# Scales of the expert weights: one per expert, surveyed one expert ahead, in place of one for all experts

## The chip, the cores and the metric

The kernel runs on one core of a Trainium2 chip. The metric is device time in microseconds (us) of one execution, lower is better. Five engines work side by side, each through its own instructions in order: PE (TensorE, matrix products; its weight loads are shown as PEld), DVE (VectorE), ACT (ScalarE), POOL (GpSimd) and SP, which here only issues DMA transfers. An instruction waits on semaphores for what it reads and for the buffers that it overwrites, and everything queued behind it on its engine waits with it.

## What is computed

Attention, a dense layer with a cosine, and a mixture of eight experts with a Sinkhorn gate, over 4 x 576 = 2304 tokens of width 512:

```python
scores = q @ k.T / 8 + decay;  x = softmax(scores, causal) @ v      # 4 x 8 heads of 64
h = x @ w_in;  x = (h * cos(h)) @ w_out                             # 512 -> 2048 -> 512
P = exp(x @ w_gate - max)                                           # 2304 x 8
for _ in range(8):
    P /= P.sum(1, keepdims=True) + 1e-9
    P /= P.sum(0, keepdims=True) + 1e-9
    P *= N / E
for e in range(8):
    out += P[:, e:e+1] * (max(x @ w1[e], 0) @ w2[e])                # 512 -> 1024 -> 512
```

## The kernel before

**Stages.** Attention fills the first 238 us, the dense layer the time to 654.7, the experts the rest. The experts' products are made of sums of submatrices (seven products in place of eight), in float16 with a high and a low part. So that the float16 parts neither overflow nor vanish, weights and activations are multiplied by powers of two: `scales["w1"]`, `scales["w2"]` for the weights of all experts together, `scales["x0"]` to `["x2"]` for the three thirds of the tokens. `backs` holds the inverses, and the last step of the gate's normalisation multiplies them into the gate.

**The survey in the dense stage.** The scale of `w1` needs the largest magnitude of all of `w1`, so both tensors are read once before the experts start: 128 chunks of 128 x 512 float32 (256 KB), loaded by `load_chunk` (L773) on SP into two buffers in turn (`seen` and `u`), and looked at by `survey` (L777, the instruction L779) on ACT: an absolute value with a running sum into one column of `found`, which bounds the magnitude from above. ACT also makes half of each sine of the dense layer. `find_scale` (L785, put in its places by `schedule_scale`, L804) reduces `found` to one number: a reduction on DVE, a transpose on PE (L791), a reduction, a product with ones on PE (L795) that spreads the number over the partitions, and four small DVE operations (L796 to L801). It takes two PSUM banks for that from three (`ps_h`, name "h") that the first products of the dense layer, L174, also use in turn. The same function serves the three thirds of the tokens.

**The experts.** Sixteen blocks follow each other: expert e = 0 to 7, and for each the two halves hb of its hidden width. A block runs over three pairs of token tiles in the order 0, 1, 2 or 2, 1, 0. A pair is two first layers (`first_layer`, L1314: seven products of six matmuls each, L1304, with one slot behind each product) and one second layer (`second_layer`, L1388: seven products of 24 matmuls, L1425, with two slots behind each). That makes 28 slots a pair and 84 a block. In a first layer three products accumulate in the same bank `y`, and ACT copies the bank to `ct` in between (L1320), while DVE adds (L1324) and forms the low parts (L1330), ACT the high parts (L1327, L1337, L1338), POOL further low parts (L1333, L1339).

**The plan.** What isn't a product of the block itself is set by hand: `put_at(n, ...)` hangs a function on slot n, counted through all blocks, and `hook()` behind each product issues what hangs there. `plan_weights` (L1472) hangs the preparation of the next block's four weight sets: `w_scale` (L1059, on ACT, in place), the sums on POOL (L1085), the high parts on ACT (L1114), the low parts on POOL (L1125), and the load of a later set on SP (`load_raw`, L1039). `plan_groups` (L1450) hangs the sums and parts of the token blocks of pairs 1 and 2 in block 0; those use four rooms `xs0` to `xs3` of 128 x 384. `keep_blocks` (L1021, slot 52 of block 0) stores the seven blocks `xc` of pair 2 to DRAM, `fetch_blocks` (L1025) brings them back behind the first layers of each block. The gate's normalisation (`sinkhorn`) is hung on the first slots of blocks 0 and 1 in small steps.

## Time and profile before

| what | us |
|---|---|
| runs | 1996.81, 1990.7, 1992.62 |
| median of the runs | 1992.62 |
| profiled execution, its own time | 1994.5 |
| its span in the profile | 1992.8 |
| granted clock of PE, mean | 0.999 |
| PE busy | 1953.8 (98%) |
| DVE, ACT, POOL busy | 1498.4, 1175.6, 1102.1 |

In the trace the dense stage runs from 238 to 654.7, block 0 from 654.7 to 746.5 (its third pair from 718.39), block 1 to 835.1; each of the blocks 3 to 15 takes 82.2 us. The names of the code appear in the rows without their numbers. A row "A x, us | idle" gives the busy time of a group, the mean time of one instruction in ns, and the idle time of its engine just before it with what ended most of it. The times in a row of the timeline are its start and its length, and in brackets stands how long the engine had been idle and what released it. A row of windows gives for one stretch the busy time of each engine with the count of its instructions, the granted clock of PE (1.00 is 2.4 GHz), the share of time that the DMA engines were busy, and GB/s.

### The profile page before, as it was taken

Reading aid. Unit: us, or ns where it says so; the run is one execution under the profiler, and the core shown is the slowest. Engines: PE = TensorE matmul, PEld = TensorE weight load, DVE = VectorE, ACT = ScalarE, POOL = GpSimd, SP = SyncE. Lnnn points to the kernel's source line nnn. Section 1 sums busy time; section 2 is a strip of 40 time slices with the busy share of each in tenths; the row PEclk is TensorE's granted clock in tenths of the full one; section 3 lists DMA queues with packets and bytes.
Section 4 is the critical chain, followed back from the end, with each engine's and each line's share of the span. In section 5 each row is a group of like instructions: output and inputs, shape, how many; then the busy total and the mean of one; then the engine's idle time right before and its main releaser. Section 6 shows DMA issues by size and latency. Waiting matters only on the chain.

```text
span 1992.8 us, 40081 instructions
## 1 busy us (share of the span) xinstructions
PE 1953.8 (98%) x15056; PEld 1544.5 (78%) x15056; DVE 1498.4 (75%) x3310; ACT 1175.6 (59%) x2481; POOL 1102.1 (55%) x1400
## 2 busy tenths in 40 slices
PE   7999999999999999999999999999999999999998
PEld 6888989898887676777777777777777777777776
DVE  8999788786666577787777777777777777777776
ACT  6888776656544675555555555655555555555543
POOL 7877455242166895555655546555465455565531
PEclk9999999999999999999999999999999999999999
DMA  5454255454321122112021120220212202122022
GB/s 124 111 111 103 67 183 171 134 157 142 97 62 45 44 88 77 49 61 88 22 78 62 48 88 27 80 72 31 88 33 77 78 22 88 33 78 78 12 88 64
DMA packets 142881, 157.58 MB, mean 79 GB/s; under 512 B 64608, under 2 KB 98784, under 8 KB 142688
## 3 DMA queue, kind: packets, MB, share of 16 engines
q1 hardware_dynamic: 142688, 155.04, 25.8%
q8 instruction: 118, 1.93, 0.4%
q14 instruction: 75, 0.61, 0.1%
HBM read 139.71 MB, written 10.37 MB: 75 GB/s over the span
## 4 chain that ended last, share of the span: by engine, by line
PE 85%; DVE 8%; ACT 3%; POOL 2%; issue 1%; DMA 0%; POOLq 0%; DVEq 0%; SPq 0%; ACTq 0%
PE y L1425 19%; PE y L1304 18%; PE bq L1425 14%; PE bq L1304 13%; PE a L829 7%; PE ph L174 6%; PE pv L598 2%; PE pst L548 2%; PE pss L491 1%; PE pss L492 1%; DVE acc L844 1%; DVE dm L134 1%; PE pv L578 1%; POOL w L135 1%; DVE xt L861 1%
## 5 line engine op out<-in xcount | busy, mean ns | idle before, releaser
L1425 PEld LDWEIGHTS <-h 128*128 128x128 f16 x6048 | 591.5, 98 | 76.1 <-POOL h L1339 1.2
L1304 PEld LDWEIGHTS <-wa 128*128 128x128 f16 x4032 | 394.8, 98 | 258.4 <-issue 5.0
L1304 PE MATMUL y<-xc,wa 128*128 128x384 f16 x2304 | 430.6, 326 | 1.8 <-ACT ct L1320 1.0
L1339 POOL TENSOR_TENSOR h<-rt,h 128x384 f16<-128x384 f32 x192 | 175.6, 915 | 452.2 <-ACT h L1338 444.9
L1425 PE MATMUL y<-wb,h 128*128 128x256 f16 x3456 | 408.9, 273 | 0.9 <-POOL h L1339 0.9
L1320 ACT ACTIVATE ct<-y 128x384 f32<-128x384 f32 x192 | 94.3, 491 | 423.1 <-PE y L1304 422.9
L1304 PE MATMUL bq<-xc,wa 128*128 128x384 f16 x1728 | 328.7, 327 | 0.2 <-ACT ct L1320 0.2
L1425 PE MATMUL bq<-wb,h 128*128 128x256 f16 x2592 | 306.7, 273 | 0.2 <-DVE h L1330 0.2
L1406 DVE SCALAR_TENSOR_TENSOR acc<-y,gate,acc 128x256 f32<-128x256 f32 x504 | 212.6, 477 | 48.6 <-PE y L1425 48.6
L829 PE MATMUL a<-H,w 128*128 128x512 f32 (+1 forms) x960 | 213.3, 370 | 4.0 <-DVE acc L844 2.6
L174 PE MATMUL ph<-xt,w 128*128 128x512 f32 (+1 forms) x960 | 211.5, 369 | 0.0
L829 PEld LDWEIGHTS a<-H,w 128*128 128x128 f32 x960 | 174.3, 188 | 30.4 <-issue 4.3
L174 PEld LDWEIGHTS ph<-xt,w 128*128 128x128 f32 x960 | 174.9, 188 | 22.8
L1406 DVE SCALAR_TENSOR_TENSOR acc<-bq,gate,acc 128x256 f32<-128x256 f32 x378 | 159.7, 478 | 39.2 <-PE bq L1425 39.1
L1330 DVE TENSOR_TENSOR h<-bq,h 128x384 f16<-128x384 f32 x288 | 158.1, 551 | 3.2 <-ACT h L1327 0.6
L1324 DVE SCALAR_TENSOR_TENSOR bq<-bq,ct 128x384 f32<-128x384 f32 x192 | 107.7, 561 | 65.4 <-PE bq L1304 64.6
L1324 DVE SCALAR_TENSOR_TENSOR bq<-y,ct 128x384 f32<-128x384 f32 x96 | 54.3, 566 | 122.8 <-PE y L1304 120.0
L1327 ACT CAST h<-bq 128x384 f16<-128x384 f32 x288 | 134.7, 483 | 14.2 <-DVE bq L1381 14.0
L1333 POOL TENSOR_TENSOR h<-st,h 128x384 f16<-128x384 f32 x96 | 88.1, 917 | 84.6 <-ACT h L1327 80.7
L194 ACT ACTIVATE t<-t,shift 128x512 f32<-128x512 f32 (+1 forms) x80 | 54.5, 681 | 89.1 <-DVE t L193 87.3
L1337 ACT ACTIVATE rt<-bq 128x384 f32<-128x384 f32 x192 | 93.8, 488 | 21.4 <-DVE bq L1324 18.8
L127 POOL TENSOR_SCALAR w<-dx 128x512 fp32r<-128x512 f32 x32 | 19.9, 623 | 154.0 <-DVE dx L126 153.1
(234 smaller groups left out, 3268.8 us busy)
## 6 DMA issues: line engine op xcount, KB each, us to landing
xc<-xd SPq DMA_DIRECT2D x105, 384.0 KB
sg<-in_moe_w_dram SPq DMA_DIRECT2D x64, 512.0 KB
seen<-in_moe_w_dram SPq DMA_DIRECT2D x64, 256.0 KB
u<-in_moe_w_dram SPq DMA_DIRECT2D x64, 256.0 KB
stg<-in_moe_w_in_dram SPq DMA_DIRECT2D x16, 512.0 KB
stg<-in_moe_w_out_dram SPq DMA_DIRECT2D x16, 512.0 KB
xd<-xc SPq DMA_DIRECT2D x14, 384.0 KB
q<-q SPq DMA_DIRECT2D x30, 160.0 KB
```

Source lines behind the costliest of these rows:

```text
L174: nc.tensor.matmul(ps[:, 0:n], w[:, ws, kk * P : (kk + 1) * P], XT[j][:, xs, kk, :], start=first, stop=kk == KD - 1 and (ws, xs) == PASSES ...
L829: nc.tensor.matmul(a_of[b, j][x][:, 0:n], w[:, s1, DM + x * P : DM + (x + 1) * P], H[:, s2, 0:n], start=i == 0 and n_ == 0, stop=end and n ...
L1304: nc.tensor.matmul(ps[:, 0:HN], w[:, ws, a, k, :], X[b][:, xs, k, :], start=fresh and n == 0, stop=n == 5, skip_group_check=not fresh,)
L1320: nc.scalar.activation(c, cut(ps), AF.Copy, scale=RAISE)
L1324: nc.vector.scalar_tensor_tensor(cut(c), cut(ps), RAISE, other, ALU.mult, ALU.add)
L1327: nc.scalar.copy(HT[m][c][:, 0, :], src)
L1330: nc.vector.tensor_tensor(HT[m][c][:, 1, :], src, HT[m][c][:, 0, :], ALU.subtract)
L1333: nc.gpsimd.tensor_tensor(HT[m][c][:, 1, :], src, HT[m][c][:, 0, :], ALU.subtract)
L1337: nc.scalar.activation(r, cut(ps), AF.Relu)
L1339: nc.gpsimd.tensor_tensor(HT[m][c][:, 1, :], r, HT[m][c][:, 0, :], ALU.subtract)
L1406: nc.vector.scalar_tensor_tensor(a, v, gate[:, tt, e : e + 1], a, ALU.mult, ALU.add)
L1425: nc.tensor.matmul(ps[:, at_ * HD : (at_ + 1) * HD], HT[m][a][:, s1, c * P : (c + 1) * P], W2T[side][m][:, s2, b, :], start=fresh and m == ...
```

## The change

Each expert has scales of its own for `w1` and `w2`. The dense stage surveys the 16 chunks of expert 0 alone; `share_most` and `set_scale` take the place of `find_scale` for the weights: the per-partition maxima (two numbers) are reduced on DVE, stored to DRAM, and read back to every partition (128 x 256 numbers), where one reduction and five small operations on DVE give the two scales and the factor that undoes them. The survey of expert e + 1 hangs on the slots of the first block of expert e: 16 looks on ACT and the loads of their chunks on SP, into the rooms `xs`, which are now two tiles of 128 x 768, of which a chunk takes 512 columns. In block 0 the looks stand on slots 53, 55, ..., 83, in the others on slots 2, 7, ..., 77. The maxima are shared at slot 2 of the block behind, the scale is set at its slot 8, and the gate's column of the expert is multiplied by the factor at its slot 10; for the experts 0 and 1 the gate's last step does it.

```diff
-        chunks = []
-        for x, src in enumerate(surveys):
-            for r in range(src.shape[0] // P):
-                chunks += [(x, src[r * P : (r + 1) * P, h, :]) for h in range(src.shape[1])]
-        NSEEN = len(chunks) // 2
...
-        scales = {nm: keep.tile([P, 1], F32, name=f"s{nm}") for nm in ("w1", "w2", "x0", "x1", "x2")}
-        backs = {nm: keep.tile([P, 1], F32, name=f"r{nm}") for nm in ("w1", "w2", "x0", "x1", "x2")}
-
-        def load_chunk(n):
-            if n < len(chunks):
-                nc.sync.dma_start(seen[n % 2], chunks[n][1])
-
-        def survey():
-            for n, (x, _) in enumerate(chunks):
-                nc.scalar.activation(
-                    seen[n % 2], seen[n % 2], AF.Abs, accum_out=found[x][:, n % NSEEN : n % NSEEN + 1]
-                )
-                load_chunk(n + 2)
+        scales = {nm: keep.tile([P, 1], F32, name=f"s{nm}") for nm in ("x0", "x1", "x2")}
+        backs = {nm: keep.tile([P, 1], F32, name=f"r{nm}") for nm in ("x0", "x1", "x2")}
+        wscale = [keep.tile([P, 2], F32, name=f"ws{x}") for x in range(2)]
+        wmost = keep.tile([P, 2], F32, name="wmost")
+        undo = keep.tile([P, NE], F32, name="undo")
+        sdram = ctx.enter_context(tc.tile_pool(name="sdram", bufs=1, space=bass.MemoryType.DRAM))
...
+        def look(e, n):
+            nc.scalar.activation(seen[n % 2], seen[n % 2], AF.Abs, accum_out=found[e % 2][:, n : n + 1])
+
+        def load_chunk(e, n):
+            if n < NSEEN:
+                nc.sync.dma_start(seen[n % 2], chunks_of(e)[n])
+
+        def survey(e):
+            for n in range(NSEEN):
+                look(e, n)
+                load_chunk(e, n + 2)
                 yield
+
+        def share_most(e, room):
+            nc.vector.tensor_reduce(
+                wmost, found[e % 2].rearrange("p (x n) -> p x n", x=2), axis=AX.X, op=ALU.max
+            )
+            nc.sync.dma_start(mostd[e], wmost)
+            nc.sync.dma_start(room, mostd[e].rearrange("p x -> (p x)").partition_broadcast(P))
+
+        def set_scale(e, room):
+            sc = wscale[e % 2]
+            nc.vector.tensor_reduce(wmost, room.rearrange("q (p x) -> q x p", x=2), axis=AX.X, op=ALU.max)
+            nc.vector.tensor_scalar(wmost, wmost, 2.0**-LIMIT, 2.0**LIMIT, ALU.max, ALU.min)
+            nc.vector.tensor_scalar(wmost.bitcast(I32), wmost.bitcast(I32), 0x7F800000, None, ALU.bitwise_and)
+            nc.vector.tensor_scalar(
+                sc.bitcast(I32), wmost.bitcast(I32), -1.0, float((254 + TOP) << 23), ALU.mult, ALU.add
+            )
+            nc.vector.tensor_scalar(wmost, wmost, 2.0**-TOP, None, ALU.mult)
+            nc.vector.scalar_tensor_tensor(
+                undo[:, e : e + 1], wmost[:, 0:1], 1.0 / RAISE, wmost[:, 1:2], ALU.mult, ALU.mult
+            )
+
+        def undo_gate(e):
+            g = gate[:, :, e]
+            nc.vector.tensor_scalar(g, g, undo[:, e : e + 1], None, ALU.mult)
...
-        load_chunk(0)
-        load_chunk(1)
-        looking[0] = survey()
-        PER = 2
-        schedule_scale("w1", found[0], NSEEN // PER + 1)
-        schedule_scale("w2", found[1], 2 * NSEEN // PER + 1, 3)
+        load_chunk(0, 0)
+        load_chunk(0, 1)
+        looking[0] = survey(0)
+        at(after_l2, 12, lambda: share_most(0, seen[0][:, 0 : 2 * P]))
+        at(after_l2, 18, lambda: set_scale(0, seen[0][:, 0 : 2 * P]))
...
-        xtmp = temps("xs", 4)
+        xs = [xp.tile([P, 2 * HN], F32, name=f"xs{c}") for c in range(2)]
+        xtmp = [t[:, c : c + HN] for t in xs for c in (0, HN)]
...
-            t, scale = stage_of(n), scales[ejobs[n][0]]
+            kind, e = ejobs[n][0:2]
+            which = 0 if kind == "w1" else 1
+            t, scale = stage_of(n), wscale[e % 2][:, which : which + 1]
...
-                    undo = small["gr"]
-                    nc.vector.scalar_tensor_tensor(undo, backs["w1"], 1.0 / RAISE, backs["w2"], ALU.mult, ALU.mult)
                     for p in range(NPR):
                         g = gate[:, p * TT : (p + 1) * TT, :]
-                        nc.vector.tensor_scalar(g, g, undo, backs[f"x{p}"], ALU.mult, ALU.mult)
+                        nc.vector.tensor_scalar(g, g, backs[f"x{p}"], None, ALU.mult)
+                    for e in range(2):
+                        undo_gate(e)
...
+        def plan_survey(blk):
+            e = blocks[blk][0] + 1
+            base = blk * NB
+            first, step = (53, 2) if blk == 0 else (2, 5)
+
+            def begin():
+                seen[:] = [t[:, 0:DM] for t in xs]
+                load_chunk(e, 0)
+                load_chunk(e, 1)
+
+            put_at(base + first - 2, begin)
+            for n in range(NSEEN):
+                put_at(base + first + step * n, lambda n=n: (look(e, n), load_chunk(e, n + 2)))
+            room = xs[0][:, DM : DM + 2 * P]
+            put_at(base + NB + 2, lambda: share_most(e, room))
+            put_at(base + NB + 8, lambda: set_scale(e, room))
+            if e > 1:
+                put_at(base + NB + 10, lambda: undo_gate(e))
...
+            if hb == 0 and e + 1 < NE:
+                plan_survey(blk)
```

On SP, around the stores of pair 2's blocks in block 0 (`xd2`; `sg` are the stages of the weights, `xs` the rooms of the survey). Before:

```order
L1046 DMA sg0_8569<-in_moe2_w1_dram 128x4x256
L1051 DMA sg1_8570<-in_moe2_w2_dram 128x2x512
L1023 DMA xd2_8593<-xc00_8533 128x1536
L1023 DMA xd2_8593<-xc01_8534 128x1536
L1023 DMA xd2_8593<-xc02_8535 128x1536
L1023 DMA xd2_8593<-xc03_8536 128x1536
L1023 DMA xd2_8593<-xc04_8538 128x1536
L1023 DMA xd2_8593<-xc05_8539 128x1536
L1023 DMA xd2_8593<-xc06_8537 128x1536
L1051 DMA sg2_8577<-in_moe2_w2_dram 128x2x512
```

And now on SP, the same place:

```order
L1085 DMA sg1_8345<-in_moe2_w2_dram 128x2x512
L787 DMA xs0_8360<-in_moe2_w1_dram 128x512
L787 DMA xs1_8361<-in_moe2_w1_dram 128x512
L1057 DMA xd2_8366<-xc00_8308 128x1536
L1057 DMA xd2_8366<-xc01_8309 128x1536
L1057 DMA xd2_8366<-xc02_8310 128x1536
L1057 DMA xd2_8366<-xc03_8311 128x1536
L1057 DMA xd2_8366<-xc04_8313 128x1536
L1057 DMA xd2_8366<-xc05_8314 128x1536
L1057 DMA xd2_8366<-xc06_8312 128x1536
L787 DMA xs0_8360<-in_moe2_w1_dram 128x512
L787 DMA xs1_8361<-in_moe2_w1_dram 128x512
```

Two chunk loads stand ahead of the seven stores, and the next two behind them.

On ACT, the start of the third pair of block 0 (`ct` are the copies of products, `h` the high parts, `wa10` the weights of the next block). Before:

```order
L1114 CAST wa10_8575<-sg2_8577 128x256
L1114 CAST wa10_8575<-tm0_8571 128x1024
L1320 ACTIVATE ct0_8540<-y_9448 128x384
L1320 ACTIVATE ct1_8541<-y_9448 128x384
L1221 ACTIVATE rs_4982<-rs_4982,eps_4988 128x18
L1320 ACTIVATE ct2_8582<-bq_9481 128x384
L1337 ACTIVATE rt0_8556<-bq_9461 128x384
L1338 ACTIVATE h00_8542<-bq_9461 128x384
```

And now on ACT:

```order
L1150 CAST wa10_8350<-sg2_8352 128x256
L783 ACTIVATE xs1_8361,found1_4991<-xs1_8361 128x512
L1150 CAST wa10_8350<-tm0_8346 128x1024
L1356 ACTIVATE ct0_8315<-y_9227 128x384
L783 ACTIVATE xs0_8360,found1_4991<-xs0_8360 128x512
L1356 ACTIVATE ct1_8316<-y_9227 128x384
L1257 ACTIVATE rs_4982<-rs_4982,eps_4988 128x18
L1356 ACTIVATE ct2_8357<-bq_9262 128x384
L1373 ACTIVATE rt0_8331<-bq_9240 128x384
L1374 ACTIVATE h00_8317<-bq_9240 128x384
L783 ACTIVATE xs1_8361,found1_4991<-xs1_8361 128x512
```

One look stands between the two copies of `y`, further ones ahead of them and behind the high parts.

On DVE, the second first layer of block 3's first pair, where the scale of expert 2 is set (`wmost` and `ws0` are the maxima and the scale). Before:

```order
L1324 SCALAR_TENSOR_TENSOR bq_11904<-bq_11904,ct1_8541 128x384
L1381 TENSOR_TENSOR bq_11868<-y_11824,st0_8573 128x384
L1330 TENSOR_TENSOR h03_8545<-bq_11850,h03_8545 128x384
L1330 TENSOR_TENSOR h05_8547<-bq_11833,h05_8547 128x384
L1324 SCALAR_TENSOR_TENSOR bq_11942<-y_11892,ct3_8589 128x384
```

And now on DVE:

```order
L1360 SCALAR_TENSOR_TENSOR bq_11754<-bq_11754,ct1_8316 128x384
L1417 TENSOR_TENSOR bq_11718<-y_11671,st0_8348 128x384
L804 TENSOR_REDUCE wmost_5001<-xs0_8360 128x2
L805 TENSOR_SCALAR wmost_5001<-wmost_5001 128x2
L806 TENSOR_SCALAR wmost_5001<-wmost_5001 128x2
L807 TENSOR_SCALAR ws0_4999<-wmost_5001 128x2
L810 TENSOR_SCALAR wmost_5001<-wmost_5001 128x2
L811 SCALAR_TENSOR_TENSOR undo_5002<-wmost_5001 128x1
L1366 TENSOR_TENSOR h03_8320<-bq_11700,h03_8320 128x384
L1366 TENSOR_TENSOR h05_8322<-bq_11680,h05_8322 128x384
L817 TENSOR_SCALAR gate_66<-gate_66,undo_5002 128x18
L1360 SCALAR_TENSOR_TENSOR bq_11799<-y_11742,ct3_8362 128x384
```

Six operations of the scale stand ahead of the low parts h03 and h05, and the scaling of the gate's column ahead of the next addition.

## Rows read from the trace of the kernel before

**Rows 1.** Windows, by stage: busy us (count) of PE, PEld, DVE, ACT, POOL; clock; DMA; GB/s.

```profile
238.00:553.00 315.00, 311.86 (x1518) 274.69 (x1517) 233.25 (x396) 203.48 (x467) 118.69 (x108) 1.00 0.48 147
835.07:1903.99 1068.92, 1068.92 (x8192) 801.36 (x8190) 791.27 (x1696) 586.95 (x1222) 589.24 (x806) 1.00 0.18 59
```

**Rows 2.** Groups of instructions, PE, 238 to 553: busy, mean ns, idle and releasers.

```profile
L829 PE MATMUL a<-H,w 128*128 128x512 f32 (+1 forms) x751 | 165.3, 368 | 3.1 <-DVE acc L844 2.6 <-DVE H L200 0.5
```

**Rows 3.** One tile, `seen`, then `u`: ns (min/median/max), first and last start, waits.

```profile
L779 ACT ACTIVATE seen<-seen x64: 620/632/672, 242.0 to 552.5; 128x512 f32<-128x512 f32 x64
L779 ACT ACTIVATION_READ_ACCUMULATOR seen<-seen x64: 183/192/241, 242.6 to 553.1; 128x1 f32 x64
...
  DMA seen<-in_moe_w_dram: 13.6, 16
...
L779 ACT ACTIVATE u<-u x64: 613/617/634, 243.2 to 554.5; 128x512 f32<-128x512 f32 x64
```

**Rows 4.** Timeline of PE around a search for a scale: start, length, instruction.

```profile
570.33 0.27 PE L791 MATMUL pl<-ident,gm 128*1 128x128 f32 x1
571.43 1.64 PE L875 MATMUL pl<-xt,wg 128*128 128x384 f32 x8 [0.83 <-DVE H L200]
```

**Rows 5.** Timelines of POOL and of SP's queue, block 0.

```profile
716.27 0.91 POOL L1196 TENSOR_TENSOR xc<-xs,xc 128x384 f16<-128x384 f32 x1
...
701.87 17.22 SPq L1023 DMA_DIRECT2D xd<-xc  x7
```

**Rows 6.** A window with a fetch of blocks, and the timeline of one chunk.

```profile
931.00:935.00 4.00, 4.00 (x39) 3.53 (x38) 3.86 (x10) 3.16 (x6) 1.84 (x2) 1.00 0.99 369
...
425.95 0.33 SPq L775 DMA_DIRECT2D seen<-in_moe_w_dram  x1
428.45 0.63 ACT L779 ACTIVATE seen<-seen 128x512 f32<-128x512 f32 x1 [0.42 <-DMA seen<-in_moe_w_dram]
```

**Rows 7.** Timelines of PE and ACT, start of block 0's third pair.

```profile
718.39 1.14 PE L1304 MATMUL y<-xc,wa 128*128 128x384 f16 x6
720.94 1.14 PE L1304 MATMUL y<-xc,wa 128*128 128x384 f16 x6 [0.30 <-ACT ct L1320]
722.89 1.14 PE L1304 MATMUL y<-xc,wa 128*128 128x384 f16 x6
...
720.41 0.48 ACT L1320 ACTIVATE ct<-y 128x384 f32<-128x384 f32 x1
```

**Rows 8.** Timelines of DVE and PE, start of block 1, and a window behind them.

```profile
745.73 4.09 DVE L1224 TENSOR_TENSOR gate<-gate,rs 128x144 f32<-128x144 f32 x1
750.32 0.39 PE L1268 MATMUL bq<-cs,ones 128*128 128x8 f32 x2 [2.65 <-DVE cs L1225]
...
751.00:755.00 4.00, 4.00 (x16) 1.97 (x14) 1.61 (x6) 0.69 (x2) 0.00 (x0) 0.57 0.00 0
```

**Rows 9.** Windows: the two halves of block 0's third pair.

```profile
718.39:732.77 14.38, 14.08 (x90) 8.61 (x88) 9.88 (x24) 10.80 (x26) 14.12 (x21) 1.00 0.19 67
732.77:746.53 13.76, 13.76 (x129) 12.33 (x126) 10.54 (x26) 8.44 (x18) 12.10 (x19) 1.00 0.22 70
```

**Rows 10.** Timeline of ACT and PE around slot 37 of block 4.

```profile
1009.97 0.47 ACT L1327 CAST h<-bq 128x384 f16<-128x384 f32 x1
1010.55 0.49 ACT L1320 ACTIVATE ct<-bq 128x384 f32<-128x384 f32 x1
1011.33 1.14 PE L1304 MATMUL bq<-xc,wa 128*128 128x384 f16 x6
```

**Rows 11.** Timelines of DVE and PE: slot 10 of block 5, and small operations.

```profile
1093.80 0.57 DVE L1324 SCALAR_TENSOR_TENSOR bq<-y,ct 128x384 f32<-128x384 f32 x1 [0.56 <-PE y L1304]
1094.52 1.14 PE L1304 MATMUL y<-xc,wa 128*128 128x384 f16 x6
...
579.40 0.15 DVE L797 TENSOR_SCALAR rw<-rw 128x1 int32<-128x1 int32 x1
...
749.86 0.41 DVE L1225 TENSOR_REDUCE cs<-gate 128x8 f32<-128x144 f32 x1
```

More of the change, by code (lines that the diff above doesn't have):

```diff
@@ L762, with chunks_of @@
         surveys = [w1.rearrange("e k (h c) -> (e k) h c", c=DM), w2.rearrange("e k (h c) -> (e k) h c", c=DM)]
-        chunks = []
-        for x, src in enumerate(surveys):
-            for r in range(src.shape[0] // P):
-                chunks += [(x, src[r * P : (r + 1) * P, h, :]) for h in range(src.shape[1])]
-        NSEEN = len(chunks) // 2
+        def chunks_of(e):
+            got = []
+            for src in surveys:
+                rows_ = src.shape[0] // (NE * P)
+                for r in range(e * rows_, (e + 1) * rows_):
+                    got += [src[r * P : (r + 1) * P, h, :] for h in range(src.shape[1])]
+            return got
@@ L768 @@
+        NSEEN = len(chunks_of(0))
         found = [keep.tile([P, NSEEN], F32, name=f"found{x}") for x in range(2)]
         largest = keep.tile([P, KD * NCH], F32, name="largest")
-        scales = {nm: keep.tile([P, 1], F32, name=f"s{nm}") for nm in ("w1", "w2", "x0", "x1", "x2")}
-        backs = {nm: keep.tile([P, 1], F32, name=f"r{nm}") for nm in ("w1", "w2", "x0", "x1", "x2")}
-        def load_chunk(n):
-            if n < len(chunks):
-                nc.sync.dma_start(seen[n % 2], chunks[n][1])
@@ new lines @@
+        wmost = keep.tile([P, 2], F32, name="wmost")
+        undo = keep.tile([P, NE], F32, name="undo")
+        sdram = ctx.enter_context(tc.tile_pool(name="sdram", bufs=1, space=bass.MemoryType.DRAM))
+        mostd = [sdram.tile([P, 2], F32, name=f"mostd{e}") for e in range(NE)]
+        def look(e, n):
[3 more added lines that the diff above has]
+                nc.sync.dma_start(seen[n % 2], chunks_of(e)[n])
```

## The prediction

> **What bounds the kernel now.** I read the windows by stage first, because a share over the whole span mixes an attention stage, a dense layer and the experts. From 835.07 to 1903.99 us TensorE (PE) has no idle time at all, with the clock at 1.00 [rows 1]: there a wait of PE for another engine is lost time, and nothing that only unloads ScalarE (ACT) or VectorE (DVE) can gain. In the dense stage, 238 to 553, PE misses 3.1 us of 315 [rows 1], and the groups of instructions put all of it on the second product, L829, waiting for DVE: 2.6 us for the addition L844 and 0.5 for L200 [rows 2]. So what leaves the dense stage can bring a few us, while what arrives in the experts meets a PE that has no gap to hide it in, only the distance between a result and the product that needs it. The working is against the profiled execution, 1994.5 us (span 1992.8); it lies 1.9 us above the median of the runs, 1992.62, and I carry the same difference to that median.
>
> **What leaves the dense stage.** 128 looks stand there now, 64 on each of two buffers, 632 and 617 ns plus a read of the accumulator of 0.19 us each [rows 3]; 16 stay. The ACT time, over 80 us, is not the gain: ACT is not what PE waits for. ACT's 13.6 us of waiting for chunks [rows 3] does delay the sine, and through it DVE now and then, but L844 also queues behind DVE's own weight splitting. Of the 3.1 us between none and all can go; I take 1.0. The two searches for a scale go as well, four small matmuls with two PSUM banks each. One stands at 570.33, and the next matmul starts at 571.43 after 0.83 us idle for L200 [rows 4]: three banks rotate, and with one taker fewer the bank in question has long been read. That gives 1.1 us. The other three I take at 0.2 us each, below the 0.27 of the one shown. **Sum 2.7 us gained, bounds 1.1 and 4.8.**
>
> **Block 0: the survey of expert 1 meets the stores of the blocks.** On SP the first two chunk loads stand ahead of the seven stores xd<-xc, and chunks 2 and 3 behind them. The second load must wait until POOL has read the last part of `xs1`; that instruction runs from 716.27 to 717.18 [rows 5]. Before, the stores went out one by one between 701.87 and 719.09 as their blocks came ready [rows 5]; now all seven queue behind that load and leave from about 717.7 on. They carry 7 x 384 KB = 2.75 MB. A stretch in which seven such blocks are fetched moves 369 GB/s at a DMA share of 0.99 [rows 6], so they take 7.5 us; with 0.9 us from issue to the first packet (half of what a chunk's 2.5 us [rows 6] hold beside its own 0.7 of data) they end near 726.1. Chunk 2 (256 KB) adds 0.7 us and some 0.3 to be seen: 727.1.
>
> ACT takes its queue in order, and look 2 stands between the two copies of a first layer's `y` (the order of ACT above). Look 2 ends at 727.1 + 0.73 = 727.8, the copy behind it (0.48 us [rows 7]) at 728.3, and the fifth product, which accumulates over what that copy reads, starts at 728.4 instead of 722.89 [rows 7]. **That is 5.5 us.** The PE does not stop at once: look 1 already shifts the copy that now starts at 720.41, and the third product with it, by about 1.1 us, which is within the 5.5; the rest, 4.4 us, is one gap before the fifth product. The ends: a chunk that overtook the stores would take the 2.5 us that a chunk takes from its issue at 425.95 to its look at 428.45 [rows 6], from an issue near 721.7, and cost 2.6 us in all; stores 40% slower would cost 8.5. I take the value at the measured rate. The Trainium skill, "DMA: Bandwidth & Descriptors", section on queues, rings and completion order, says that descriptors of one ring are consumed in ring order; by it chunk 2 cannot overtake and the term is 5.5, and no row shown here tests it.
>
> After the PE has stood for 2.65 us at 750.32 the granted clock averages 0.57 from 751 to 755, that is, mostly the lower level, 1.2 GHz [rows 8]: 0.43 x 4 = 1.7 us more. A gap of 4.4 us should bring the same, **1.7 us** (nothing in the low case). The remaining looks of block 0 come every second slot, 1.95 us apart. ACT is busy 10.80 of 14.38 and 8.44 of 13.76 us in the two halves of that pair [rows 9], so 8.9 us are free, against 14 looks x 0.73 = 10.2; 0.73 is 632 + 192 ns less the 0.1 by which neighbours overlap. About 1.3 us do not fit, and the gap itself gives ACT room: **1.0 us**, bounds 0 and 2.5.
>
> **Six steady surveys** (experts 2 to 7, blocks 2, 4 to 12). Half of the 16 looks stand in second layers, where ACT runs ahead; they cost nothing while it does, and up to 0.7 each where it does not. Of the eight in first layers the tight one stands at slot 37, the tenth of its pair. Now the cast at 1009.97 is followed by the copy at 1010.55, which ends at 1011.04; the product that needs it starts at 1011.33 [rows 10], a margin of 0.29. With a look after the cast (1010.37 to 1011.10) the copy ends at 1011.59, 0.3 us late. Slot 7 loses less than 0.1 in the same way; the other six stand where the next copy has more time. **0.4 x 6 = 2.4 us**, bounds 0 and 0.8 x 6.
>
> The new scale on DVE stands at slot 8 of the next block: one reduction over 256 numbers (a reduction of 144 in steps took 0.41 us, so 0.45), five small operations and, two slots on, the scaling of a gate column, each 0.19 us from start to start (0.15 for an operation such as that at 579.40 [rows 11], and the step to the next): 0.45 + 6 x 0.19 = 1.6 us. DVE idles 0.56 us before the addition at 1093.80, which ends at 1094.37, and the product that accumulates over what it read starts at 1094.52 [rows 11]: 0.71 us are there. The rest is 0.9; a little overlap between neighbours gives back 0.1: **0.8 x 6 = 4.8 us**, and 0.4 for expert 1, whose scale falls among the steps of the gate's normalisation. Bounds: 0.1 x 6 (the operations all fall into idle time) and 1.5 x 6 (none does).
>
> One row speaks for the upper end: at 745.73 a multiplication on DVE took 4.09 us beside POOL's weight work [rows 8], where a reduction over the same 144 numbers took 0.41 [rows 11]. The Trainium skill, "SBUF — State Buffer", section on the two separate sides, has a rule for it that speaks against this change: DVE and GpSimd take a shared port pair in turns, the whole instruction long, when DVE has two SBUF inputs or uses two ports; by it `undo`, and perhaps the small operations beside it, could each wait for a POOL instruction. The small one at 579.40 took 0.15 us [rows 11], so the sum stays without it.
>
> **What costs nothing.** The maxima go to DRAM and back: two transfers of about 2.5 us [rows 6], 5.0 together, between slot 2 (DVE free near 2.8 us after the block's start) and the scale at slot 8 (DVE there at 10.3 us): 7.5 us of cover. Without it DVE, in order, would wait for the landing, and every us beyond would be PE's. On SP the round trip holds a weight load that is needed dozens of slots later. The loads of chunk 4 stand ahead of the fetch of seven blocks and hold it some 4.6 us; its blocks are read two pairs on, 40 us later. 29 MB of chunk reads move into a stage with a DMA share of 0.18 [rows 1]. Scales and gates are otherwise as many operations as before.
>
> **Sum.** -2.7 + 5.5 + 1.7 + 1.0 + 2.4 + 4.8 + 0.4 = +13.1. Against the profiled execution 1994.5 + 13.1 = 2007.6; on the median 1992.62 + 13.1 = **2005.7 us**.
>
> **The rivals.**
> 1. *Faster: the experts absorb the survey.* If ACT and DVE run far enough ahead that no product waits for a look or a scale, and chunk 2 lands before its look, only the gain of 2.7 is left, and with the other timing on POOL the 4.09 us multiplication need not recur: 2.65 of gap and 1.7 of clock. 1992.6 - 2.7 - 4.4 = 1985.5. For it: ACT idles 8.9 us in that pair [rows 9]. Against: the margin of 0.29 before an accumulating product [rows 10] is smaller than a look, and the load of chunk 1 cannot go before 717.2 [rows 5]. It decides for "faster" as long as the experts lose under about 1 us. Chance 0.10.
> 2. *No change: the chunk costs little.* Chunk 2 overtakes the stores (2.6, no drop of the clock), the multiplication does not recur (-4.4), the steady surveys cost half (3.8) and the rest of block 0 1.0: 1992.6 - 2.7 + 2.6 - 4.4 + 3.8 + 1.0 = 1992.9. For it: nothing forces the collision at 745.73 to return. Chance 0.20.
> 3. *Slower still: DVE waits at slot 8.* If the round trip of 8-byte rows takes 9 us instead of 5, or POOL holds DVE during the scale, each of six scales costs about 1.5 us more: 2005.7 + 9 = 2014.7. For it: the 4.09 us row [rows 8]. Against: the cover of 7.5 us. Chance 0.12.
> The forecast itself has 0.58.
>
> **How the numbers follow.** 0.3%, 6 us, is about what a measurement of this kernel can tell from no change. Slower by more holds the forecast and rival 3: 0.70. Within it: rival 2, 0.20. Faster: rival 1, 0.10. The forecast's own range is 1999 to 2012. The whole range, 1991 to 2014, takes in most of rival 2 and the lower part of rival 3, and leaves out rival 1 and the tail above.
>
> **What would show it.** Right: in the new profile PE has a gap of some 4 us near 724 that ends on a copy of `y` on ACT behind a look that waited for a chunk; a granted clock near 0.5 behind it; in each odd block from 3 on a gap of about 0.8 us before the fourteenth product, released by DVE; in each even block from 2 on gaps of some 0.3 us released by ACT; L829 idle near 2 us in the dense stage. Wrong: no idle PE in the steady blocks, or chunk 2 landing before 724, or DVE waiting for the broadcast maxima. If the dense stage gained more than 5 us, ACT had been its limit after all, and my reading of rows 2 would be at fault.

## The result

The changed kernel took 2020.74 us (median of 4 runs) against 1992.61, a ratio of 1.0138 with a 95% interval of 1.0120 to 1.0155: slower by 28 us, where the forecast was slower by 13. Run once more later beside other kernels (below) it took 2014.24, a ratio of 1.0106, 1.0089 to 1.0123. One run of this repeat, of 7159.17 us, and one of a later version, of 3368.41, are left out of the ratios; the medians without them are 2013.94 here and 1992.79 there. The direction held, the size did not, and the first result lies outside the range.

The profiled execution is the one of 2020.45 us (span 2018.7, mean granted clock 0.995). Laid beside the one of before by the starts of the blocks in the PE timeline, in us:

| stretch | before | after | difference | forecast |
|---|---|---|---|---|
| up to the experts | 654.72 | 653.37 | -1.35 | -2.7 |
| block 0 | 91.81 | 101.21 | +9.4 | +8.2 |
| block 1 | 88.54 | 88.92 | +0.4 | +0.4 |
| blocks 2, 4, ..., 12 (looks) | 493.44 | 494.67 | +1.2 | +2.4 |
| blocks 3, 5, ..., 13 (new scale) | 493.27 | 509.52 | **+16.3** | +4.8 |

The windows by stage and the group of the second product in the dense stage, of the changed kernel (columns as in [rows 1] and [rows 2]):

```profile
238.00:553.00 315.00, 309.92 (x1508) 273.11 (x1507) 235.40 (x396) 134.05 (x245) 128.17 (x123) 1.00 0.20 58
835.07:1929.91 1094.84, 1082.73 (x8270) 810.31 (x8268) 806.79 (x1759) 640.14 (x1418) 595.10 (x817) 1.00 0.26 82
...
L863 PE MATMUL a<-H,w 128*128 128x512 f32 (+1 forms) x744 | 163.7, 368 | 5.1 <-DVE acc L878 4.5 <-DVE H L200 0.5
```

ACT fell from 203 to 134 us in the dense stage and PE gained nothing from it there; its idle time before the second product rose from 3.1 to 5.1. In the experts PE now has 12 us of idle where it had none.

**Dense stage.** One gap is new. DVE sets expert 0's scale there, and two of its small operations end with an instruction of POOL (timelines of DVE, POOL and PE, changed kernel):

```profile
328.25 1.14 DVE L805 TENSOR_SCALAR wmost<-wmost 128x2 f32<-128x2 f32 x1
329.63 0.89 DVE L807 TENSOR_SCALAR ws<-wmost 128x2 int32<-128x2 int32 x1
...
328.05 1.31 POOL L135 TENSOR_TENSOR w<-dx,dm 128x512 fp32r<-128x512 f32 x1 [0.72 <-DVE dm L134]
329.44 1.05 POOL L121 TENSOR_TENSOR dm<-stg 128x512 f32<-128x512 f32 x1
...
334.94 0.41 PE L863 MATMUL a<-H,w 128*128 128x384 f32 x1 [2.38 <-DVE acc L878]
```

328.25 + 1.14 = 329.39 beside 328.05 + 1.31 = 329.36, and 330.52 beside 330.49. DVE spends 3.1 us on the scale and comes late to the addition L878, and PE stands 2.38 us where before it stood 0.42.

**Block 0** went as written down (timelines of SP's queue, ACT and PE, and the window behind the gap):

```profile
709.22 6.96 SPq L787 DMA_DIRECT2D xs<-in_moe_w_dram  x2
716.24 6.16 SPq L1057 DMA_DIRECT2D xd<-xc  x7
722.50 8.10 SPq L787 DMA_DIRECT2D xs<-in_moe_w_dram  x4
...
727.20 0.63 ACT L783 ACTIVATE xs<-xs 128x512 f32<-128x512 f32 x1 [6.16 <-DMA xs<-in_moe_w_dram]
...
728.35 2.08 PE L1340 MATMUL y<-xc,wa 128*128 128x384 f16 x6 [5.15 <-ACT ct L1356]
...
728.35:732.35 4.00, 4.00 (x14) 2.15 (x14) 1.55 (x4) 3.11 (x9) 2.43 (x4) 0.50 0.48 129
```

The seven stores queue behind the second chunk's load, the third chunk behind them; its look (L783, the survey's instruction) starts at 727.20, PE stands 5.15 us, and the clock behind it is 0.50, the level of 1.2 GHz.

**Block 1** changed the reason of its loss, and in this profile not its length (in the repeat it took 90.98): the multiplication that took 4.09 us [rows 8] is short, and a copy on ACT behind looks is late (timelines of DVE and PE):

```profile
753.78 0.61 DVE L1260 TENSOR_TENSOR gate<-gate,rs 128x144 f32<-128x144 f32 x1
...
759.70 1.59 PE L1340 MATMUL y<-xc,wa 128*128 128x384 f16 x6 [2.87 <-ACT ct L1356]
```

**Block 5**, one of the six in which a scale is set (timelines of SP's queue, DVE, POOL and PE, then the windows behind the gap in block 5 and behind the one in block 9):

```profile
1095.01 0.33 SPq L799 DMA_DIRECT2D mostd<-wmost  x1
1097.79 0.33 SPq L800 DMA_DIRECT2D xs<-mostd  x1
...
1103.51 0.42 DVE L804 TENSOR_REDUCE wmost<-xs 128x2 f32<-128x256 f32 x1 [1.00 <-DMA xs<-mostd]
1104.57 0.81 DVE L810 TENSOR_SCALAR wmost<-wmost 128x2 f32<-128x2 f32 x1
...
1104.44 0.91 POOL L1375 TENSOR_TENSOR h<-rt,h 128x384 f16<-128x384 f32 x1 [2.06 <-ACT h L1374]
...
1107.17 1.14 PE L1340 MATMUL y<-xc,wa 128*128 128x384 f16 x6 [2.21 <-DVE bq L1360]
...
1107.17:1111.17 4.00, 4.00 (x22) 2.72 (x22) 2.93 (x6) 3.19 (x8) 1.69 (x2) 0.65 0.94 344
1444.23:1448.23 4.00, 4.00 (x34) 3.30 (x34) 3.86 (x9) 3.18 (x8) 1.68 (x2) 1.00 0.91 331
```

Store, wait, read back: from the store's issue at 1095.01 to DVE's reduction at 1103.51 it takes 8.5 us, where I had put two transfers of 2.5. DVE idles 1.00 us for it, and one of the small operations then lasts until POOL's instruction is over (1105.38 and 1105.35). The accumulating product waits 2.21 us. The gaps in blocks 9, 11 and 13 are as long, and the clock behind the one in block 9 stays at 1.00, while it averages 0.65 over 4 us in block 5.

### The profile page after: what moved, and what is told of

The parts are those of the page before. It is cut to its first block, busy times and chain, and to the rows that moved or that the text cites. A ratio compares the mean times of both kernels' runs of the same rounds, so it can differ in the third digit from the quotient of the medians.

```text
span 2018.7 us, 40136 instructions
## 1 busy us (share of the span) xinstructions
PE 1960.8 (97%) x15050; PEld 1547.0 (77%) x15050; DVE 1506.4 (75%) x3361; ACT 1166.1 (58%) x2481; POOL 1099.3 (54%) x1400
## 4 chain that ended last, share of the span: by engine, by line
PE 80%; DVE 8%; DMA 3%; POOL 3%; ACT 3%; issue 2%; DVEq 0%; POOLq 0%; SPq 0%; ACTq 0%
PE y L1461 18%; PE y L1340 16%; PE bq L1461 13%; PE bq L1340 12%; PE a L863 7%; PE ph L174 7%; PE pv L598 2%; DMA xs<-mostd 2%; PE pst L548 2%; PE pss L491 1%; PE pss L492 1%; DMA mostd<-wmost 1%; DMA xs<-in_moe_w_dram 1%; DVE dm L134 1%; DVE acc L878 1%
## 5 line engine op out<-in xcount | busy, mean ns | idle before, releaser
L1366 DVE TENSOR_TENSOR h<-bq,h 128x384 f16<-128x384 f32 x288 | 157.2, 549 | 6.9 <-ACT h L1363 4.9
```

The costliest lines, as they stand in the source:

```text
L1366: nc.vector.tensor_tensor(HT[m][c][:, 1, :], src, HT[m][c][:, 0, :], ALU.subtract)
```

## The experiments

Two questions were open after the profile: is it the scale at slot 8 at all, and what of it, the arrival of the maxima or the operations. Line numbers shift by a few lines between these kernels; where a time of a block is given, it is the distance between starts in the PE timeline.

**Scale at slot 15.**

```diff
-            put_at(base + NB + 8, lambda: set_scale(e, room))
+            put_at(base + NB + 15, lambda: set_scale(e, room))
-                put_at(base + NB + 10, lambda: undo_gate(e))
+                put_at(base + NB + 18, lambda: undo_gate(e))
```

> The changed kernel with the new scale set at slot 15 of the next block (in the second layer, two slots ahead of the first use) in place of slot 8, and the gate's column scaled at slot 18 in place of 10. Theory A, the scale at slot 8 holds DVE and DVE holds the accumulating product: the gaps of 1.1 to 2.2 us in blocks 3, 5, 7, 9, 11 and 13, and the clock lost behind two of them, go; these blocks took 83.4, 86.3, 86.1, 84.6, 84.6 and 84.6 us and fall to about 82.2, together 16 us: 2004.5. Theory B, the looks on ACT and the chunks' traffic slow these blocks wherever the scale stands: within 3 us of 2020.7.

Measured 2004.1 (1.0063, 1.0047 to 1.0080). The six blocks took 494.26 us together, 1.0 more than before, and no gap over 0.3 us is left in them. Theory A holds, B falls: the looks and the chunks' traffic were there as before.

**Maxima shared early.**

```diff
-            put_at(base + NB + 2, lambda: share_most(e, room))
+            put_at(base + NB + (-4 if blk else 2), lambda: share_most(e, room))
```

> The changed kernel with the maxima shared at slot 80 of the block of the survey (three slots behind its last look) in place of slot 2 of the next block, in the six steady blocks; the scale stays at slot 8. Theory A1, the late arrival of the maxima is what counts: DVE no longer waits for them and the gaps fall under 0.4 us, about 14 us less: 2006. Theory A2, the arrival (0.5 to 0.9 us of DVE's idling) is the smaller part and the seven operations of 0.2 to 0.9 us stay in the path: gaps of 0.8 to 1.5 us remain, the clock no longer falls behind them: 7 to 8 us less, 2013. In both, small operations of DVE that start while POOL runs an instruction end with it.

Measured 2011.32 (1.0098). All six blocks took 83.33 us, each with the same gap. Block 5 (timelines of DVE, POOL, PE):

```profile
1101.78 0.41 DVE L804 TENSOR_REDUCE wmost<-xs 128x2 f32<-128x256 f32 x1
1104.05 0.71 DVE L817 TENSOR_SCALAR gate<-gate,undo 128x18 f32<-128x18 f32 x1
...
1103.81 0.91 POOL L1375 TENSOR_TENSOR h<-rt,h 128x384 f16<-128x384 f32 x1 [2.06 <-ACT h L1374]
...
1105.28 0.48 PE L1340 MATMUL y<-xc,wa 128*128 128x384 f16 x2 [0.95 <-DVE bq L1360]
```

The reduction now starts straight behind DVE's work, 10.3 us after the block's start. The reduction and the five small operations are through before POOL's instruction begins; the scaling of the gate's column is caught by it instead and lasts 0.71 in place of 0.23 us. That leaves 1.1 us a block, 6.7 in all, which is the operations' own price: A2 for this part, and the other 9.6 of the 16.3 is arrival with what follows from it.

**Four more small operations**, added to the run just shown:

```diff
             nc.vector.tensor_scalar(wmost, wmost, 2.0**-TOP, None, ALU.mult)
+            for _ in range(4 if e > 1 else 0):
+                nc.vector.tensor_scalar(wmost, wmost, 1.0, None, ALU.mult)
```

> The run with the maxima shared early (2011.3, gaps of 0.95 us) with four more small operations on DVE ahead of the one that makes the factor, 0.2 us each, for the experts 2 to 7; the numbers stay what they are. Theory P, a small DVE operation that starts while POOL's instruction of 0.91 us runs ends with it: now an operation ahead of the two low parts starts inside it, in place of the scaling of the gate's column behind them, and the two low parts of 1.0 us together come after POOL's end: gaps of 2.0 to 2.2 us, 6 to 8 us more, 2018. Theory N, only the length counts: gaps of 1.3 us, 2 us more, 2013.

Measured 2018.69 (1.0132). Block 5 (timelines of DVE, POOL, PE):

```profile
1105.54 0.88 DVE L813 SCALAR_TENSOR_TENSOR undo<-wmost 128x1 f32<-128x1 f32 x1
...
1105.49 0.91 POOL L1377 TENSOR_TENSOR h<-rt,h 128x384 f16<-128x384 f32 x1 [2.06 <-ACT h L1376]
...
1108.02 0.48 PE L1342 MATMUL y<-xc,wa 128*128 128x384 f16 x2 [2.01 <-DVE bq L1362]
```

0.82 us of operations made the gap 1.06 us longer, in all six blocks to 2.01: theory P. The operation that starts 0.05 us after POOL's ends 0.02 us after it. Five blocks took 84.39 us, and one 86.04 with a gap of the same 2.01: there the clock fell, in the others it did not.

**Later, by one slot and by three.** The share at slot 3, and at slot 5:

```diff
-            put_at(base + NB + 2, lambda: share_most(e, room))
+            put_at(base + NB + (3 if blk else 2), lambda: share_most(e, room))
```

> The changed kernel with the maxima shared at slot 3 in place of slot 2 of the block behind, in the six steady blocks; nothing else. Theory A1, the arrival of the maxima stands last at slot 8: they arrive 0.98 us later, each gap before the accumulating product grows from 1.1 to 2.2 to about 3 us, and the clock falls behind more of them: 6 to 13 us more than the changed kernel, 2026 to 2034. Theory A2, the operations are what counts and the arrival only by chance: within 2 us of 2020.7.

> The changed kernel with the maxima shared at slot 5 in place of slot 2, in the six steady blocks, which unlike slot 3 should move the reduction behind the first additions of the block, by about 2 us. Theory A1, arrival: the maxima come near 13 us after the block's start, the gaps grow to 3 to 3.6 us and the clock falls behind some: 2026 to 2036. Theory A2, the operations alone, wherever the maxima come: within 2 us of the changed kernel beside it.

Slot 3 measured 2012.11 and moved nothing: the reduction stood 2.70 us after the block's start, as with slot 2, since both slots lead to the same place behind DVE's queue. So it says nothing of a delay; it is a repeat. In five of the six blocks DVE began to read the maxima 10.6 to 10.9 us after the block's start, and these took 83.3 to 83.5 us; in block 11 it was at 11.2, and that block took 84.4. Slot 5 does move the reduction, by 3.8 us and not by the 2 that I had counted, and measured 2051.12 (1.0293), above both ranges. Block 5 (timelines of DVE and PE):

```profile
1114.84 0.42 DVE L804 TENSOR_REDUCE wmost<-xs 128x2 f32<-128x256 f32 x1 [4.86 <-DMA xs<-mostd]
...
1117.86 0.48 PE L1340 MATMUL y<-xc,wa 128*128 128x384 f16 x1 [5.43 <-DVE bq L1360]
```

3.86 us later at the reduction than in the changed kernel's block 5 (15.25 against 11.39 from the block's start) makes the gap 3.2 us longer, nearly one for one. A1 holds for an arrival past some 10.7 us; between 10.3, where DVE is ready, and 10.7 the wait for POOL covers it, and the blocks take 83.33 us either way.

**The changed kernel once more.**

> The changed kernel itself once more, beside the next two runs. In its first profile the maxima came 10.8 to 11.3 us after the block's start and the gaps were 1.1 to 2.2 us; with the sharing hung on slot 3 the reduction stood at the same 2.7 us, the maxima came at 10.6 to 11.1, and the gaps were 1.0 to 2.0, 2012. If the half microsecond belongs to the kernel (its order of transfers), 2019 to 2022 again. If it belongs to the chip or the placement in memory, it differs here: 2010 to 2015.

Measured 2014.24, with three of its runs between 2013.3 and 2014.5, where the first four lay between 2019.9 and 2021.2. Block 5 of this profile (timelines of DVE and PE):

```profile
1105.14 0.42 DVE L804 TENSOR_REDUCE wmost<-xs 128x2 f32<-128x256 f32 x1 [0.66 <-DMA xs<-mostd]
...
1108.17 0.65 PE L1340 MATMUL y<-xc,wa 128*128 128x384 f16 x3 [1.24 <-DVE bq L1360]
```

Over the six blocks DVE begins the reduction 10.53 to 11.05 us after the block's start, against 10.87 to 11.39 in the first profile, and the blocks take 500.4 against 509.5 us. So 9 us of these blocks go with 0.05 to 0.7 us, 0.5 in the mean, of a DRAM round trip. That so little does so much has a reason in the rows: the wait of PE does not grow evenly with the arrival, it has a step. With the reduction at 11.05 (block 5 above) the gap is 1.24 us; at 11.19 it is 2.01, because one of the five small operations now starts inside POOL's instruction and lasts to its end, and the low parts wait behind it (timelines of DVE, POOL and PE, block 11 of the run with slot 3):

```profile
1602.28 0.79 DVE L811 SCALAR_TENSOR_TENSOR undo<-wmost 128x1 f32<-128x1 f32 x1
...
1602.14 0.91 POOL L1375 TENSOR_TENSOR h<-rt,h 128x384 f16<-128x384 f32 x1 [2.06 <-ACT h L1374]
...
1604.67 0.32 PE L1340 MATMUL y<-xc,wa 128*128 128x384 f16 x1 [2.01 <-DVE bq L1360]
```

In the first profile five of the six blocks lie past that step, and behind two of them the clock fell, 1.7 us each; in the repeat none does. The half microsecond does not belong to the order of the instructions; chip, memory placement or something else, these runs don't tell.

**A row of its own for every partition.** The store goes to the head of 128 rows of 1 KB, and each partition reads its row; the rest of the rows was filled in the dense stage:

```diff
+            nc.sync.dma_start(mostd[e][:, 0:2], wmost)
...
-            nc.sync.dma_start(room, mostd[e].rearrange("p x -> (p x)").partition_broadcast(P))
+                nc.sync.dma_start(room, mostd[e])
```

> The changed kernel in which, for the experts 2 to 7, every partition reads back a row of its own of 1 KB, its two maxima and 254 numbers that were stored in the dense stage, in place of all reading the same 1 KB. The size, the packets and the waits are the same; left out is that the partitions share one scale. Theory C, 128 packets that read the same 1 KB are slow (3.0 us from first to last in block 5, 2.5 us in the dense stage with nothing beside them): the data are there 1.5 to 2.5 us earlier, DVE doesn't wait, and the gaps fall to the 0.95 us of the run with the maxima shared early: 2011. Theory D, the weight load and the fetch behind it in the queue slow the packets: they stay at about 3 us, 2020.

Measured 2011.75 (1.0106), all six blocks at 83.33 us, the same as with the maxima shared early: the data were there in time. SP's queue and the window of the read alone, then, of the changed kernel, the window of a read of one shared 1 KB in the dense stage:

```profile
1259.81 0.33 SPq L799 DMA_DIRECT2D mostd<-wmost  x1
1261.21 0.33 SPq L803 DMA_DIRECT2D xs<-mostd  x1
...
1262.15:1262.75 0.60, 0.60 (x5) 0.36 (x4) 0.48 (x1) 0.21 (x2) 0.40 (x1) 1.00 0.76 191
```

```profile
302.60:305.15 2.55, 2.55 (x14) 2.32 (x13) 2.43 (x4) 0.76 (x3) 1.85 (x2) 1.00 0.79 58
```

The trace's packets say it most plainly. Reading one shared KB, in block 5 of the changed kernel, 128 packets of 1 KB ran from 1100.07 to 1103.05 with a median of 193 ns each, and in the dense stage, with next to nothing beside them, from 302.61 to 305.15 with 145 ns; reading a row each, in block 7 of this run, from 1262.16 to 1263.01 with 46 ns. And the read could be issued 1.40 us after the store where it was 2.78: storing 8-byte pieces into one KB also takes longer to be confirmed than storing them 1 KB apart. A third part is the time from the read's issue to its first packet, 2.28 us in that block 5 and 0.95 here. Theory C. The three together are 1.4 + 1.3 + 2.1 = 4.8 us of the 8.5, and the remaining 3.7 is less than the 5.0 that I had counted. This run spreads the store and the read at once, so it doesn't tell how much of the read's part comes from sharing the KB and how much from how it was stored.

**Expert 1 surveyed in the dense stage, and the chunk loads behind the stores**, two ways to undo block 0:

```diff
-            if hb == 0 and e + 1 < NE:
+            if hb == 0 and 0 < e and e + 1 < NE:
...
-        looking[0] = survey(0)
+        looking[0] = survey(0, 1)
...
+            at(after_l2, 22 + x, lambda x=x: share_most(x, rooms[x]))
+            at(after_l2, 28 + 2 * x, lambda x=x: set_scale(x, rooms[x]))
```

> The changed kernel with the 16 chunks of expert 1 surveyed in the dense stage too, behind those of expert 0, and both scales set there; block 0 has no survey. If the chunk that lands behind seven stores is what block 0 lost (gaps of 1.8 and 5.15 us and a clock of 0.5 behind them), block 0 falls from 101.2 to about 92 us: 2011, less or more by 2 for the two scales in the dense stage and by 4 if the long multiplication at the start of block 1 comes back. If block 0 lost its time otherwise (another order on POOL and SP), it stays near 2020.

```diff
-            put_at(base + first - 2, begin)
+            put_at(base + (first - 2 if blk else 53), begin)
...
-                put_at(base + first + step * n, lambda ...
+                put_at(base + (first + step * n if blk else 58 + 3 * n // 2), lambda ...
```

> The changed kernel with the first two chunk loads of block 0 behind the seven stores on SP in place of ahead of them, and its 16 looks on slots 58 to 80 in steps of 1.5 slots in place of 53 to 83 in steps of 2. If the stores were held back by the second chunk's buffer and the third chunk stood behind them, the stores now leave as their blocks come ready, a chunk lands some 2.5 us from its issue, and the gap of 5.15 us shrinks to under 1: block 0 near 93 to 95 us, 2013. If chunk loads are slow there in themselves (4.7 us from the issue to the landing), ACT waits for most chunks and block 0 stays above 98 us: over 2017.

The first measured 2002.77 (1.0053): block 0 is back at 91.81 us to the hundredth. It fell 8 us further than expected for reasons outside block 0: block 1 took 2.3 us less and the six blocks 8.1 less, because the maxima were read earlier here as well (10.6 to 11.2 us), and in the dense stage no operation of the scales met POOL at its new place. The gap of 2.38 us there is 0.42 again, and the experts start at 652.07, 2.65 us before those of the kernel before:

```profile
333.19 0.41 PE L865 MATMUL a<-H,w 128*128 128x384 f32 x1 [0.42 <-DVE acc L880]
```

The second measured 2008.08 (1.0084) with block 0 at 94.51. That is 5 us under what was written down, for the same reason outside block 0: the six blocks took 503.3 us. The stores leave one by one again, and the longest gap left in the pair is below 1 us (SP's queue, PE):

```profile
701.03 17.21 SPq L1057 DMA_DIRECT2D xd<-xc  x7
...
732.69 0.48 PE L1340 MATMUL bq<-xc,wa 128*128 128x384 f16 x2 [0.96 <-ACT ct L1356]
```

**Both repairs together**, and with them the gate's normalisation at the start of block 1 a little later:

```diff
-            steps += [(x + 2) * NS + c for c in (0, 1, 2, 3, 5, 6, 22, 25)]
+            steps += [(x + 2) * NS + c for c in ((2, 3, 4, 5, 7, 8, 22, 25) if x == 1 else (0, 1, 2, 3, 5, 6, 22, 25))]
```

> Both repairs together: experts 0 and 1 surveyed in the dense stage and the later scales set at slot 15. By the blocks of the two runs: the start of the experts at 652.1, block 0 91.8 us, block 1 86 to 88.5, blocks 2 to 14 82.2 to 82.8, together 1.5 us less than the profiled run of the kernel before: 1992, against 1991.4 no difference that can be told. If the looks or the small operations cost more once nothing else holds PE, 1995.

> The same, with the six steps of the gate's normalisation at the start of block 1 one or two slots later (at 2, 3, 4, 5, 7, 8 in place of 0, 1, 2, 3, 5, 6). PE then doesn't wait 2.65 us for the column sums behind the multiplication of 4.09 us on DVE: 2.5 us less than the run before it, 1989.5. If the same multiplication holds the first additions of the block instead, nothing is gained.

> The kernel before with nothing but the six steps of the gate's normalisation at the start of block 1 one or two slots later, as in the second repaired kernel, which came out at 1990.2 against 1990.6. If those steps alone made the repaired kernel as fast as the kernel before, this run lies 1.5 to 3.5 us under the kernel before, and the change with both repairs is worth nothing or costs a little. If the repaired survey gains by itself, this run stays within 1 us of the kernel before.

The first measured 1993.48 (1.0007, 0.9998 to 1.0016), the second 1990.17 (0.9993, 0.9984 to 1.0002); the kernel before stood at 1990.57 beside them. In the second, PE waits 0.69 us for the column sums where it waited 2.65 [rows 8]:

```profile
747.56 0.36 PE L1308 MATMUL y<-cs,ones 128*128 128x8 f32 x2 [0.69 <-DVE cs L1265]
```

The same step in the kernel before alone measured 1991.40 against 1993.39 (0.9991, 0.9983 to 1.0000). So the repaired survey can't be told from none: by the profiles its experts start 2.8 us earlier than those of the kernel before (651.88 against 654.72; 655.59 with the same step alone, whose code up to there is that of the kernel before), and their 16 blocks take 1.9 us longer than with the same step alone (1330.07 against 1328.19). No version beats the kernel before by more than the measurement can tell.

## Why the prediction was wrong

**What failed: the round trip under "What costs nothing".** I priced the store and the read back at 2.5 us each, by the row of a 256 KB chunk [rows 6], set 7.5 us of cover against 5.0 and wrote zero. The trace has 8.5 us, and DVE waited for the broadcast maxima, which I had named as a sign of being wrong. A transfer with 128 pieces of 8 bytes, and one that reads the same KB 128 times, had no row, and I took the row of another shape as if it were a bound. For pieces and rows 1 KB apart 5.0 would have been too much (3.7); for these shapes it was too little. By the profiles the change cost 25.9 us where I had 13.1; 11.5 of the difference stand in the six blocks with a new scale (16.3 against 4.8), and of these 16.3 the run with the maxima shared early takes 9.6 away.

My rival 3 had the mechanism ("if the round trip of 8-byte rows takes 9 us instead of 5, or POOL holds DVE"), a price of 1.5 us a scale and a chance of 0.12. In the first profile the scales cost 1.9 us each beyond the forecast, because both of its conditions came together and the clock fell behind two gaps. That the repeat, 2014.24, ends beside its 2014.7 is chance: there the six blocks lost 7.1 us, 2.3 more than the forecast and not 9, and another 4.2 came from a dense stage that gained 0.5 in place of 2.7 and a block 1 that lost 2.4 in place of 0.4. Had I bounded this term from both sides like the others, the rival would have weighed more.

**What was set aside: DVE and POOL.** The Trainium skill, "SBUF — State Buffer", section "SBUF: two separate sides", says that whichever of the two starts first holds the shared ports for its whole instruction, when DVE's operation is in a two-port mode or has two SBUF inputs. I let one small operation of 0.15 us at 579.40 [rows 11] outvote it. It met no instruction of POOL, and it has one column and one input; operations of that shape take the same 0.15 us in the middle of one (timelines of DVE and POOL, kernel before):

```profile
679.48 0.15 DVE L797 TENSOR_SCALAR rx<-rx 128x1 int32<-128x1 int32 x1
...
678.97 0.90 POOL L1196 TENSOR_TENSOR xc<-tm,xc 128x384 f16<-128x384 f32 x1
```

The new operations have two columns or more, or, for `undo`, two inputs, and no row of such a shape stood in [rows 11]. In the twelve profiles with the new scale 113 of them start inside an instruction of POOL, and none ends before it: 1.14 and 0.89 us in the dense stage, 0.81 in block 5, 0.71 with the maxima early, 0.88 with the added operations. For these the trace agrees with the page. The low parts L1366, which read one operand from PSUM, did not wait.

**The scale's operations, 0.8 us each:** the right order. With the maxima in time a block costs 1.1 us; 0.48 of that (0.71 against 0.23) is the wait for POOL.

**Block 0, 8.2 us:** right in mechanism and near in size. The third chunk's look was to end at 727.8 and ended at 727.83, with experts that start 1.35 us earlier; by the packets of the trace the stores ran from 717.68 to 725.24, 7.6 us where I wrote 7.5, and the packets of the chunk began only at 724.82, so it did not overtake them; the gap was 5.15 us where I wrote 4.4, with the clock at 0.50 behind it. The block lost 9.4 us. With no survey in it all of that comes back, with the loads behind the stores 6.7 of it.

**Dense stage, -2.7 us:** the sum was there (2.65 us with the scales set elsewhere), though not its parts: the 1.0 for the looks did not come (PE's idle time from 238 to 553 is 3.3 us there against 3.1 before), and the two searches, which I had put at 1.7, gave 2.9: 0.6 around the one at 407 and 2.3 around the one at 570. I had also counted no cost for setting expert 0's scale in the same stage: its gap is 2.0 us longer, and the experts start 1.3 us later than with the scales set elsewhere (2.2 in the repeat). The searches' gap at 571.43 [rows 4] is gone, as written.

**Block 1, 0.4 us:** right by chance. The multiplication of 4.09 us [rows 8] took 0.61 here, as rival 1 allowed, and its gap was replaced by one of 2.87 us at 759.70, where ACT's copies stood behind looks that waited for chunks.

**Steady looks, 2.4 us:** 1.2. Blocks 4 to 12 lost 0.16 us each, before the third product behind the look at slot 37, where I had put most of the loss; the look moved the copy there by 0.39 us, where I had worked out 0.55. The rows that I read it from [rows 10] stand 28 slots earlier, at the same place of the block's first pair.

**The clock** was counted as sure behind a gap of 4 us and was so at 728.35. Behind gaps of 2 us it is not: the same 2.0 to 2.2 us lowered it in blocks 5 and 7 and not in 9, 11 and 13 of one profile. Nor is it behind the 2.65 us from which I took the price [rows 8]: the same gap in the first kernel with both repairs, 2.63 us at 747.45, left the clock at 1.00.

## What to carry to other kernels

A small transfer is not cheap because it is small: price a round trip through DRAM by a row of the same shape, or bound it widely where there is none, and put its reader behind other work rather than at the first place where the data may be there. In a stage where PE has no gap, an operation that several engines can hold up belongs where nothing accumulates behind it: seven slots later, the same work cost 0.2 us a block in place of 1.1 to 4. And a sum that says "hidden, zero" deserves the same care as the largest term, since it was the one that was wrong. The shape counts for a small operation too: the row of an operation with one column said nothing of one with two.

## What the runs showed of the hardware

- 128 reads of 1 KB from one and the same KB of DRAM, stored just before in pieces of 8 bytes, took 2.0 to 3.3 us in all in the two profiles of the changed kernel (medians of 142 to 220 ns a packet in the first); from 128 rows of their own 0.7 to 1.2 us (46 ns).
- After storing 128 pieces of 8 bytes into one KB, the queue went on 2.7 to 3.2 us after the issue, and the first packet of the read behind it came 1.2 to 2.3 us after its own; with the pieces 1 KB apart 1.40 and 0.95.
- A DVE operation of 128x2 or 128x18 within SBUF, or of 128x1 with two inputs, that starts during a POOL instruction lasts to its end (0.05 us after the start of POOL's 0.91 us: 0.88). One of 128x1 with one input does not wait (0.15 us in the middle of POOL's 0.90), nor does one that reads an operand from PSUM (0.55).
- The same kernel on two occasions had its maxima 0.05 to 0.7 us apart in the six blocks, and these blocks 9.1 us. What sets the half microsecond stays open.
- Behind equal gaps of 2.0 us PE's clock fell to the lower level in one of six blocks and not in five, behind 2.65 us at the start of block 1 in the kernel before and not in the first kernel with both repairs. What decides it stays open.
